# Loading one weight matrix in one transfer of whole rows instead of three transfers by columns

## The chip, the cores and the metric

The kernel runs on one core of a Trainium2 chip. The core has five engines with an instruction stream each: TensorE (PE; its weight loads are shown apart as PEld), VectorE (DVE), ScalarE (ACT), GpSimd (POOL) and SyncE (SP), and 16 DMA engines that all transfers share. The metric is the device time of one launch in microseconds (us). Lower is better.

## What is computed

Sliding-window attention with four sink positions, and then a feed-forward layer that takes the larger of three products:

```python
# q, k, v: (4, 8, 768, 64) float32; n_sink = 4, window = 128
scores = q @ k.T / sqrt(64)
keep = (pos_k < n_sink) | (0 <= pos_q - pos_k < window)
a = softmax(where(keep, scores, -1e9))
x = (a @ v) as (3072, 512)                  # batch and position by heads
h = maximum(maximum(x @ w1, x @ w2), x @ w3)   # w1, w2, w3: (512, 768)
out = h @ w_out                             # w_out: (768, 512), out: (3072, 512) float32
```

## The kernel before

The work is cut into 12 chunks of 256 positions, three to each batch entry. In the code a chunk is `ci`, from 0 to 11. Every chunk goes through the same steps: load q, k and v (`load`, float32, issued on SP), cast them to bf16 on ACT, DVE or POOL (`cast_qk`, `cast_v`), turn q and k so that the head dimension lies on the partitions (`turn`: four TensorE transposes into a PSUM bank and one copy out of it), `score`, `expo`, `mask`, `av`, turn the result (`xpose`), the feed-forward products `ffn_h(ci, fp, wi)` and the last product `ffn_y`. In `ffn_h`, `wi` is the weight matrix (0, 1, 2) and `fp` is the third of its 768 columns: columns 256·fp to 256·fp+255, eight matmuls of 128x256 each.

Nothing schedules this at run time. Lines 626 to 936 write out one order of calls by hand, and every engine executes its own instructions in that order. An engine whose next instruction waits for something executes nothing behind it.

Three things feed the stretch that the change touches.

- **Weights** come in on POOL (`load_w`, line 289). POOL's transfers cast float32 to bf16 on the way, and the weight in memory is 512 rows of 768 columns, so a third of the columns is 512 pieces of 256 float32 (1 KB read, 512 B written). Weights 0, 1 and 2 take three such transfers each, nine in all; `load_wo` brings w_out in two.
- **q, k, v** come in on SP, in pieces of 512 B (two positions of one head). Chunk 2's k and q are loaded in two halves by heads (`part=0`, `part=1`), which are 512 pieces each; its v is 1024.
- **Gates.** `gate=after(wi, c)` and `gate=pool_gate` put a 1x1 instruction on POOL that touches the tile to be loaded, so SP's transfer waits until POOL has reached that place (with `after`, also until that weight has landed).

Around the change the calls stand in this order (lines 697 to 739, the ones that matter): `load(2,'k')` in two halves, `load(2,'q')` in two halves, the loads of weight 2, `ffn_h(0, ...)`, `av(1, ...)`, `load(2,'v')`, `ffn_h(0, fp, 1)`, then

```python
        cast_qk(2, 'k', 1, nc.gpsimd)      # needs the second half of chunk 2's k
        ffn_h(1, 2, 0)
        cast_qk(2, 'k', 0, nc.scalar)      # needs the first half
        ffn_h(1, 0, 0)
        ffn_h(1, 1, 0)
        load_wo()                          # POOL, behind its cast of k
        load(3, 'q', gate=after(2, 300))
        ...
        turn(2, 'k', 0, nc.vector)
        ffn_h(1, 0, 1)
        turn(2, 'k', 1, nc.scalar)
        ffn_h(1, 1, 1)
        ...
        ffn_h(1, 2, 1)
        ffn_h(1, 1, 2)                     # first use of weight 2
```

TensorE takes the two `turn(2, 'k', ...)` at their places between the products, whether or not anything later is ready.

Of the kernel before, what the change touches and what calls it, by code (L numbers as in the profile page):

```python
# [16 lines left out]
def kernel(  # L17
# [31 lines left out]
    with tc.manual_schedule():  # L49
# [43 lines left out]
        def load(ci, what="kqv", gate=None, part=None, parts=1, eng=None):  # L93
            if ci >= NCH:
                return
            b, c = divmod(ci, CPB)
            t0 = c * 256
            for w in what:
                src = {"k": k, "q": q, "v": v}[w]
                if (ci, w) not in raws:  # L100
                    raws[ci, w] = raw.tile([128, H, 2, D], F32, tag=w + "_raw", name=w + "_raw")
                dst = raws[ci, w]
                if gate is not None:
                    gate(dst[0:1, 0, 0, 0:1])
                n = H // parts
                for g in range(parts) if part is None else (part,):
                    (eng or nc.sync).dma_start(
                        out=dst[:, n * g:n * g + n],
                        in_=src[b, n * g:n * g + n, t0:t0 + 256]
                            .rearrange("h (p i) d -> p h (i d)", i=2))  # L110
# [178 lines left out]
        def load_w(wi, c0=0, c1=None):  # L289
            c1 = d_ff if c1 is None else c1  # L290
            w = (moe_w1, moe_w2, moe_w3)[wi]
            nc.gpsimd.dma_start(out=w_sb[wi][:, :, c0:c1],  # L292
                                in_=w.rearrange("(a p) f -> p a f", p=128)[:, :, c0:c1])
# [98 lines left out]
        def expo(ci, p):  # L392
            if ci >= NEW:
                return expo4(ci, p)
            lo = 0 if ci % CPB else 1
            e, st = es[ci, p]
            for a in range(2):
                nc.scalar.activation(e[:, a, lo:], st[a][:, lo:], AF.Exp, scale=scale)  # L398
                give(st[a])

        def mask(ci, p, eng=None):
            if ci >= NEW:
                return mask4(ci, p)
            lo = 0 if ci % CPB else 1
            e = es[ci, p][0]
            (eng or nc.vector).tensor_mul(e[:, :, lo:], e[:, :, lo:], msk0[0] if lo else msk)  # L406
# [295 lines left out]
        score(1, (2,))  # L702
        load(2, 'q', part=1, parts=2)
        load(2, 'q', part=0, parts=2, gate=pool_gate)
        load_w(2, 0, 256)
        expo(1, 2)
        load_w(2, 256, 512)
        load_w(2, 512, 768)
        mask(1, 3)
        ffn_h(0, 1, 0)  # L710
        mask(1, 2)
# [269 lines left out]
```

## Time and profile before

| what | us |
|---|---|
| median of three runs | 175.97 |
| the three runs | 175.69, 175.97, 176.78 |
| the profiled execution's own time | 175.3 |
| its span (first to last event on the core) | 173.6 |
| TensorE busy in that span | 167.1 |
| GpSimd busy | 110.9 |

The span is 1.7 us shorter than the profiled execution's time; that remainder lies around the program. In the profile, "idle before, <- releaser" says how long an engine stood before an instruction and what ended the wait. A wait for several things is put down to the one that came last by the profile; where the engine named had long been done, it was another, often a DMA. Queue q0 (software) carries the transfers that POOL issues, queue q1 (hardware) those that SP and ACT issue. Sizes of packets are counted on the written side, so a weight piece of 1 KB counts as 512 B.

### The profile page before, as it was taken

The page shows a single profiled execution, that of the slowest core. Times are in us where ns is not written, and L with a number is a line of the kernel's source. Part 1 is how long each engine was busy: PE and PEld are TensorE (multiplying, and loading weights), DVE is VectorE, ACT ScalarE, POOL GpSimd, SP SyncE. Part 2 cuts the span into 40 slices and gives each one's busy share as a digit, 9 for nine tenths or more (in the row PEclk, how much of TensorE's full clock was granted, in tenths as well). Part 3 has the DMA queues.
Part 4 walks back from the last instruction along what each step waited for, and adds up shares of the span by engine and source line. Part 5 has one row for each costly group of instructions (what it writes and reads, how often), then busy time and mean ns, then how long its engine had stood idle before and what let it go on. Part 6 is the DMA issues. An engine that isn't in the chain of part 4 may idle for free.

```text
span 173.6 us, 5416 instructions
## 1 busy us (share of the span) xinstructions
PE 167.1 (96%) x2225; PEld 128.6 (74%) x2225; DVE 124.7 (72%) x262; ACT 88.7 (51%) x183; POOL 110.9 (64%) x193
## 2 busy tenths in 40 slices
PE   7979999999999999999999999999999999999992
PEld 2546888857696697797797797797797896896871
DVE  3387854796797985986877976877777776776361
ACT  4778544677954614817726717717636516510210
POOL 7399507545499999999999999999998600000000
PEclk9999999999999999999999999999999999999999
DMA  4999999999999997988999999989999119017303
GB/s 139 301 288 198 218 217 256 221 306 276 280 195 216 190 273 124 245 199 216 253 199 252 195 224 246 265 168 227 264 195 259 32 33 377 21 34 272 121 2 121
DMA packets 71545, 35.22 MB, mean 203 GB/s; under 512 B 27488, under 2 KB 69984, under 8 KB 71520
## 3 DMA queue, kind: packets, MB, share of 16 engines
q1 hardware_dynamic: 65824, 31.60, 79.0%
q0 software_dynamic: 5552, 3.15, 12.7%
q8 instruction: 17, 0.28, 0.7%
q10 hardware_dynamic: 144, 0.13, 0.2%
q14 instruction: 8, 0.07, 0.1%
HBM read 25.17 MB, written 6.29 MB: 181 GB/s over the span
## 4 chain that ended last, share of the span: by engine, by line
PE 85%; DMA 7%; POOL 5%; issue 1%; DVE 0%; POOLq 0%; SPq 0%
PE h_ps L517 52%; PE y_ps L564 11%; PE y_ps L540 7%; PE o L471 6%; DMA w<-in_moe_w_dram 4%; PE st L357 3%; DMA v_raw<-in_v_dram 3%; PE st L331 2%; POOL w L292 2%; POOL vb L123 1%; PE pt L138 1%; PE o L453 1%; PE y_ps L586 1%; PE sk L423 1%; POOL q_bf L118 0%
## 5 line engine op out<-in xcount | busy, mean ns | idle before, releaser
L517 PE MATMUL h_ps<-xT,w 128*128 128x256 bf16 x864 | 101.2, 273 | 0.2 <-DMA w<-in_moe_w_dram 0.2
L517 PEld LDWEIGHTS <-w 128*128 128x128 bf16 x864 | 81.7, 98 | 10.7 <-issue 0.5
L527 DVE TENSOR_TENSOR h_sb<-h_sb,h_ps 128x512 bf16<-128x512 bf16 (+1 forms) x74 | 49.0, 670 | 17.4 <-PE h_ps L517 15.6
L523 ACT CAST h_sb<-h_ps 128x512 bf16<-128x512 f32 x35 | 20.6, 589 | 51.3 <-PE h_ps L517 51.2
L129 POOL CAST vb<-v_raw 32x512 bf16<-32x512 f32 x48 | 36.8, 766 | 2.5 <-DMA v_raw<-in_v_dram 0.3
L90 POOL CAST k_bf<-k_raw 32x512 bf16<-32x512 f32 x48 | 29.6, 616 | 2.2
L398 ACT ACTIVATE e_sb<-st 128x512 bf16<-128x512 f32 (+1 forms) x48 | 23.1, 583 | 1.1 <-PE st L331 1.1
L479 DVE TENSOR_TENSOR x_sb<-o,rc 128x256 bf16<-128x256 f32 x48 | 20.4, 424 | 1.7
L564 PE MATMUL y_ps<-wo,h_sb 64*64 64x512 bf16 (+1 forms) x312 | 21.1, 377 | 0.0
L471 PE MATMUL o<-vb,e_sb 128*128 128x65 bf16 x352 | 16.5, 193 | 0.8 <-DVE vb L123 0.8
L471 PEld LDWEIGHTS <-e_sb 128*128 128x128 bf16 x352 | 14.5, 97 | 3.1 <-ACT e_sb L398 1.0
L123 POOL CAST vb<-v_raw 64x512 bf16<-64x512 f32 x18 | 12.6, 697 | 5.7 <-DMA v_raw<-in_v_dram 5.1
L389 DVE TENSOR_TENSOR e_sb<-e_part,msk 128x1024 bf16<-128x1024 bf16 x16 | 13.1, 831 | 3.3 <-ACT e_part L374 3.1
L406 DVE TENSOR_TENSOR e_sb<-e_sb,msk 128x1024 bf16<-128x1024 bf16 (+1 forms) x18 | 13.6, 776 | 2.3 <-ACT e_sb L398 2.1
L564 PEld LDWEIGHTS <-h_sb 64*64 64x64 bf16 (+1 forms) x312 | 9.9, 106 | 5.0
L374 ACT ACTIVATE e_part<-st 128x384 bf16<-128x384 f32 x32 | 13.1, 495 | 0.5 <-PE st L357 0.5
L540 PE MATMUL y_ps<-wo,h_sb 128*128 128x512 bf16 x54 | 12.8, 380 | 0.0
L476 DVE RECIPROCAL rc<-o 128x4 f32<-128x4 f32 x48 | 8.4, 174 | 4.0 <-PE o L471 3.8
L118 POOL CAST k_bf<-k_raw 128x512 bf16<-128x512 f32 x6 | 3.8, 650 | 9.5 <-PE pt L138 6.8
L118 ACT CAST q_bf<-q_raw 128x512 bf16<-128x512 f32 x13 | 7.6, 620 | 3.0 <-DMA q_raw<-in_q_dram 3.0
L540 PEld LDWEIGHTS <-h_sb 128*128 128x128 bf16 x54 | 4.8, 98 | 5.4 <-DVE h_sb L527 0.8
L427 ACT ACTIVATE e_sink<-sk 128x256 bf16<-128x256 f32 x8 | 3.1, 389 | 10.0 <-PE sk L423 10.0
(90 smaller groups left out, 142.9 us busy)
## 6 DMA issues: line engine op xcount, KB each, us to landing
k_raw<-in_k_dram SPq DMA_DIRECT2D x11, 512.0 KB, 5.6
v_raw<-in_v_dram SPq DMA_DIRECT2D x11, 512.0 KB, 5.6
q_raw<-in_q_dram SPq DMA_DIRECT2D x10, 512.0 KB, 6.9
out_dram<-y_sb SPq DMA_DIRECT2D x9, 512.0 KB, 3.1
w<-in_moe_w_dram POOLq DMA_DIRECT2D x9, 256.0 KB, 6.1
q_raw<-in_q_dram SPq DMA_DIRECT2D x4, 256.0 KB, 7.6
out_dram<-y_sb SPq DMA_DIRECT2D x1, 1024.0 KB, 5.3
wo<-in_moe_w_out_dram POOLq DMA_DIRECT2D x2, 384.0 KB, 8.0
```

What stands on the lines that cost most here:

```text
L90: f(bfs[ci, "k"][x:x + 32, :, n], raws[ci, "k"][y:y + 32, :, i].rearrange("q (p a) d -> q p a d", a=2))
L123: eng.tensor_copy(vb[ci % RING][64 * i:64 * i + 64, n, :, 0:D], raws[ci, "v"][64 * n:64 * n + 64, :, i])
L129: eng.tensor_copy(vb[ci % RING][x:x + 32, n, :, 0:D], raws[ci, "v"][y:y + 32, :, i])
L398: nc.scalar.activation(e[:, a, lo:], st[a][:, lo:], AF.Exp, scale=scale)
L406: (eng or nc.vector).tensor_mul(e[:, :, lo:], e[:, :, lo:], msk0[0] if lo else msk)
L471: nc.tensor.matmul(o[:, t, a], lhsT=e[:, a, s], rhs=vb[cv % RING][:, n, 2 * p + a], start=first, stop=True, skip_group_check=True)
L479: nc.vector.tensor_mul(xs[ci][:, p], o[:, :, :, 0:D], rc.unsqueeze(3).to_broadcast([128, 2, 2, D]))
L517: nc.tensor.matmul(hp[:, f].rearrange("q (i t r) -> q i t r", i=2, r=x.shape[3]), lhsT=w_sb[wi][:, ds, c0:c0 + 128], rhs=x, start=(ds == 0 ...
L523: (nc.scalar.copy if eng is nc.scalar else eng.tensor_copy)(dst, hp)
L527: nc.vector.tensor_max(dst[:, x], dst[:, x], hp[:, x])
L540: nc.tensor.matmul(yp, lhsT=hs[ci][:, fb, t * 128:(t + 1) * 128], rhs=wo[:, fb], start=(fb == 0), stop=(fb == FB - 1))
L564: nc.tensor.matmul(yps[ci][t][c:c + cols], lhsT=hs[ci][hp, fb, x:x + cols], rhs=wo[hp, fb], start=(turn == 0 and fb == 0), stop=(turn == 1 ...
```

## The change

Weight 2 is loaded by one transfer of all 768 columns, at the place in the order where its first third was issued. The other two issues are gone. Weights 0 and 1 and all else stay as they were.

```diff
         load(2, 'q', part=1, parts=2)
         load(2, 'q', part=0, parts=2, gate=pool_gate)
-        load_w(2, 0, 256)
+        load_w(2)
         expo(1, 2)
-        load_w(2, 256, 512)
-        load_w(2, 512, 768)
         mask(1, 3)
         ffn_h(0, 1, 0)
         mask(1, 2)
```

The transfer is now 512 pieces of 768 float32 (3 KB read, 1.5 KB written) where it was 1536 pieces of 1 KB read. The bytes are the same.

On POOL's queue, at the place behind the gate of chunk 2's q (`w_109` is weight 2, `w_107` weight 0; in brackets the counters that an instruction waits for, DMAHW for transfers of SP, DMASW for those of POOL):

```order
 L602 CAST k_raw<-w_107 1x1 [waits DMAHW1_49,DMASW1_49]
 L606 MEMSET q_raw 1x1 [waits DMAHW0_49]
-L292 DMA w_109<-in_moe_w_dram 128x4x256 x2
-L292 DMA w_109<-in_moe_w_dram 128x4x256 [waits DMASW0_49]
+L292 DMA w_109<-in_moe_w_dram 128x4x768
 L602 CAST v_raw<-w_107 1x1 [waits DVE_49]
 L118 CAST k_bf<-k_raw 128x2x2x2x64 [waits DMAHW1_49,PE_49,Pool_49]
 L300 DMA wo<-in_moe_w_out_dram 128x3x512
-L300 DMA wo<-in_moe_w_out_dram 128x3x512 [waits DMASW2_49]
-L602 CAST q_raw<-w_109 1x1 [waits DMASW7_49,Activation_49]
+L300 DMA wo<-in_moe_w_out_dram 128x3x512 [waits DMASW0_49]
+L602 CAST q_raw<-w_109 1x1 [waits DMASW6_49,Activation_49]
```

Two issues go, and everything behind them keeps its order: the gate of chunk 2's v, the cast of the second half of chunk 2's k, the two loads of w_out, the gate of chunk 3's q.

On TensorE, at its first weight load from weight 2 (`ffn_h(1, 1, 2)`):

```order
 L517 LDWEIGHTS w_108
 L517 MATMUL h_ps<-xT,w_108 128x256
-L517 LDWEIGHTS w_109 [waits DMASW7_49]
+L517 LDWEIGHTS w_109 [waits DMASW6_49]
 L517 MATMUL h_ps<-xT,w_109 128x256 [waits PE_49]
 L517 LDWEIGHTS w_109
```

The order of TensorE's instructions is unchanged. Its first use of weight 2 waited for the second of the three transfers, and waits for the one transfer now.

## Prediction

> **What bounds the kernel now.** I read the page's totals and slices first, then the busy time by stages, then the timeline around the change, then single transfers.
>
> ```profile
> span 173.6 us, 5416 instructions
> PE 167.1 (96%) x2225; PEld 128.6 (74%) x2225; DVE 124.7 (72%) x262; ACT 88.7 (51%) x183; POOL 110.9 (64%) x193
> PE   7979999999999999999999999999999999999992
> DMA  4999999999999997988999999989999119017303
> PE 85%; DMA 7%; POOL 5%; issue 1%; DVE 0%; POOLq 0%; SPq 0%
> ```
>
> TensorE is the bound: 96% busy and 85% of the chain that ended last. But the DMA engines are near full as well, from the second slice to the 31st. The stages (columns: stretch, length, busy of PE, PEld, DVE, ACT, POOL, granted clock) show where TensorE has room:
>
> ```profile
> 9.00:15.80 6.80, 5.33 (x88) 3.44 (x86) 5.78 (x16) 5.23 (x12) 6.42 (x11) 1.00 1.29 253
> 22.70:26.40 3.70, 3.67 (x35) 3.28 (x36) 1.48 (x3) 2.08 (x4) 0.00 (x0) 1.00 1.30 216
> 26.40:30.40 4.00, 4.00 (x43) 3.49 (x41) 1.80 (x3) 1.79 (x3) 3.27 (x6) 1.00 1.25 260
> 60.00:170.00 110.00, 110.00 (x1587) 88.49 (x1585) 81.89 (x161) 49.52 (x105) 72.42 (x108) 1.00 0.82 187
> ```
>
> From 22.7 us TensorE has no gap worth naming, so there is next to nothing to win behind that point, and a wait put in there is not made good later: it moves the end by its whole length. The granted clock is 1.00 in every stage, also in the one where TensorE stood for 1.47 us (6.80 - 5.33), so I price no slower clock for a wait of that length.
>
> The timeline of TensorE's weight loads, with POOL and ACT beside them, shows which inputs arrive just in time:
>
> ```profile
> 22.73 3.39 PEld L517 LDWEIGHTS <-w 128*128 128x128 bf16 x32 [0.34 <-DMA w<-in_moe_w_dram]
> 26.13 0.32 PEld L138 LDWEIGHTS <-k_bf 128*128 128x128 bf16 x4
> 27.39 0.23 PEld L138 LDWEIGHTS <-k_bf 128*128 128x128 bf16 x4 [0.17 <-POOL k_bf L118]
> 27.57 2.56 PEld L517 LDWEIGHTS <-w 128*128 128x128 bf16 x24
> 25.17 0.62 ACT L118 CAST k_bf<-k_raw 128x512 bf16<-128x512 f32 x1
> 17.53 2.23 POOL L292 DMA_DIRECT2D w<-in_moe_w_dram  x3
> 26.72 0.61 POOL L118 CAST k_bf<-k_raw 128x512 bf16<-128x512 f32 x1 [6.81 <-PE pt L138]
> 27.28 1.51 POOL L300 DMA_DIRECT2D wo<-in_moe_w_out_dram  x2
> ```
>
> The transposes at 27.39, `turn(2, 'k', 1)`, wait for POOL's cast, which ends at 27.33. That cast had POOL idle for 6.81 us before it. The row blames TensorE's transposes, but the cast stands ahead of chunk 2's transposes in the order and can only wait for those that last used the buffer, long done. So it was the load, and the single transfers bear that out (start from the timeline, last number: us to landing):
>
> ```profile
> 16.59 0.74 POOL L292 DMA_DIRECT2D w<-in_moe_w_dram  x1
> w<-in_moe_w_dram POOLq DMA_DIRECT2D x1, 256.0 KB, 6.1
> w<-in_moe_w_dram POOLq DMA_DIRECT2D x1, 256.0 KB, 7.6
> 17.58 0.92 SPq L107 DMA_DIRECT2D k_raw<-in_k_dram  x2
> k_raw<-in_k_dram SPq DMA_DIRECT2D x1, 256.0 KB, 6.5
> 17.99 0.51 SPq L107 DMA_DIRECT2D k_raw<-in_k_dram  x1
> k_raw<-in_k_dram SPq DMA_DIRECT2D x1, 256.0 KB, 8.6
> 18.27 0.75 POOL L292 DMA_DIRECT2D w<-in_moe_w_dram  x1
> w<-in_moe_w_dram POOLq DMA_DIRECT2D x1, 256.0 KB, 9.7
> ```
>
> The last third of weight 1 (16.59) lands at 22.69, which is what TensorE waits for at 22.73. The thirds of weight 2 start landing at 17.53 + 7.6 = 25.1, the second at 18.27 + 9.7 = 28.0. Chunk 2's k lands at 17.58 + 6.5 = 24.1 (first half) and 17.99 + 8.6 = 26.6 (second half). 26.6 is 0.13 us ahead of POOL's cast at 26.72. **The second half of chunk 2's k is on TensorE's path with about no slack**, and it shares the DMA engines with weight 2.
>
> How they share is in the queues' packets, in windows of 7, 2, 1.2 and 3 us:
>
> ```profile
> q0 software_dynamic: 2720, 1.35, 143.6%
> q0 software_dynamic: 429, 0.22, 77.7%
> q1 hardware_dynamic: 420, 0.21, 52.0%
> q0 software_dynamic: 170, 0.17, 84.1%
> q1 hardware_dynamic: 170, 0.09, 35.3%
> q1 hardware_dynamic: 1730, 0.87, 116.1%
> q0 software_dynamic: 5552, 3.15, 12.7%
> ```
>
> From 13 to 20 us weights run alone: 7000 x 16 / 2720 = 41.2 ns for one piece of 1 KB on one DMA engine. From 22 to 24 us weight 2 and chunk 2's k run together, 429 packets against 420. From 33 to 34.2 us it is w_out with pieces of 2 KB (1 KB written) against the q and k loads: 170 against 170. So the queues take turns **by pieces, whatever their size**. A turn of both costs 2000 x 16 / 424.5 = 75.4 ns with 1 KB pieces and 1200 x 16 / 170 = 112.9 ns with 2 KB pieces. Queue q1 alone (9 to 12 us) takes 3000 x 16 / 1730 = 27.7 ns a piece. The last row, for the whole span, shows pieces uncut: 9 transfers x 512 + 2 x 384 + 11 x 16 (one completion per DMA engine) is 5552 exactly, with w_out's 2 KB pieces counted once.
>
> **The change, part by part.**
>
> *Two issues fewer on POOL.* Three cost 2.23 us, one 0.74 or so: 1.5 us less. POOL then stands idle before its cast of k anyway (6.81 us), and the gate of chunk 2's v, which comes 1.5 us sooner, is followed on SP by a transfer that stands behind the two loads of q. Gain: nothing. If that idle time were gone it would be 1.5 us of POOL's time.
>
> *Weight 2 lands sooner.* It is first needed by `ffn_h(1, 1, 2)`, the last 8 of the 24 weight loads from 27.57, so at about 27.57 + 16 x 0.107 = 29.3 (2.56 / 24 = 0.107); today its second third is there at 28.0. No row shows TensorE waiting for weight 2. Gain: nothing. The gate of chunk 3's q, which now needs the whole weight, is reached at 28.8, behind the landing worked out below.
>
> *Weight 2 takes a larger share while k is on its way.* This is the price. Each DMA engine has 32 pieces of weight 2 (512 / 16) where it had 96, and every turn moves 3 KB instead of 1. No row shows 3 KB pieces; going on from 75.4 and 112.9 ns by the same 37.5 ns per KB, a turn of both takes 150.4 ns. From below, the third KB could be free: 112.9. From above, pieces might cost more the longer they are: three lone 1 KB pieces plus one of q1 make 3 x 41.2 + 27.7 = 151.3, and nothing in the rows goes past that; I allow 170. I take 150.4, with both ends kept.
>
> Clock from 22.69, when the last DMA engine is done with weight 1 (its landing). Check on today: weight 2's first third is 32 turns x 75.4 ns = 2.41 us, landing at 25.10; the row says 25.1. The second half of k lands 26.59 - 22.69 = 3.90 us after that point, so 3.90 / 0.0754 = 51.7 pieces of k go out from there (32 of the second half and some 20 of the first). After the change the first 32 of these take their turns with 3 KB pieces, the rest run alone:
>
> 32 x 150.4 ns + 19.7 x 27.7 ns = 4.81 + 0.55 = 5.36 us, landing at 28.05, **1.46 us later**. Weight 2 itself lands at 22.69 + 4.81 = 27.5 instead of 30.4.
>
> POOL's cast follows at 28.18, ends at 28.79, and the transposes start at 28.85 instead of 27.39: TensorE stands still for 1.46 us. The first half of k lands 1.39 us after that point today, which is 18.4 turns, so it lands at 22.69 + 18.4 x 0.150 = 25.46 instead of 24.1; ACT's cast goes from 25.17 to about 25.6 and ends at 26.2, which TensorE meets at 26.13: up to 0.15 us, which is part of the 1.46, since the later wait is for a fixed moment. Behind POOL's cast the issue of w_out and the gate of chunk 3's q move by the same 1.46 us, and so does everything on TensorE that needs them. Behind the one transfer the loads of q and v have the DMA engines to themselves and catch up: the next half of q lands at 28.05 + 32 x 0.0277 = 28.9; it landed at 18.54 + 10.4 = 28.9 before.
>
> ```profile
> 18.54 1.89 SPq L107 DMA_DIRECT2D q_raw<-in_q_dram  x2
> q_raw<-in_q_dram SPq DMA_DIRECT2D x1, 256.0 KB, 10.4
> ```
>
> Nothing behind that is late against TensorE, and TensorE has no gap in which to win it back. Sum: 0 (POOL) + 0 (weight 2 sooner) + 1.46 = **+1.46 us**, 0.8%. On the profiled execution that is 173.6 + 1.46 = 175.1 of span and 175.3 + 1.46 = 176.8 of time; its own time lies 0.7 us below the median of the runs, 175.97, so the median after is **177.4 us**.
>
> On how the turns are taken, the Trainium skill (DMA: Bandwidth & Descriptors, section "Queues, rings and completion order") says that a DMA engine goes round its queues by whole packets of some 9 to 17 descriptors. The counts above are equal either way, so the rows cannot tell packets from single pieces. Even if all 32 pieces of weight 2 went ahead of k, the second half of k would still have all of them in front of it, and the sum stays what it is.
>
> **The rivals.**
>
> *Not slower: the long rows are cut.* If the transfer is split into pieces of at most 1 or 2 KB read, or the queues share by bytes, k keeps its turns, lands at 26.6, and nothing changes: 176.0. Against it stands the count of 5552, in which 2 KB pieces are whole; for it, that no row shows a longer one. It decides wherever a turn stays under 113 ns, for then k is late by only 0.3 us.
>
> *A gain: one large transfer is cheaper.* What could be won is the wait for weight 1's end (0.34) only if weight 2 were out of its way, which it isn't, and the 0.17 us before the transposes: 175.7 at best. Against it: 2 KB pieces cost 112.9 - 27.7 = 85 ns where two of 1 KB cost 82. The Trainium skill (same page, "Rules for kernel authors") asks for transfers of 1 MiB and more, and its fit of 2.0 us plus bytes over 436 GB/s would estimate one transfer of 1.5 MiB at 5.6 us against 9.6 for three in a row. Here, whatever is saved on weight 2 finds nobody waiting for it.
>
> *Heavier: a 3 KB piece costs more than the line through 1 and 2 KB says.* At 170 ns a turn, 32 x 170 + 19.7 x 27.7 = 5.99 us, k lands at 28.7, 2.1 us later: 178.1. From 160 ns on the loss passes 1%.
>
> *Heavier: w_out is late too.* It is issued behind the cast, at 28.7 instead of 27.3. If its second half then takes all its turns against chunk 3's q (24 x 33 ns = 0.8 us more), half a microsecond of that may reach TensorE: 1.46 + 0.5, 177.9.
>
> **How the numbers follow.** The forecast (+1.1 to +1.9 around 1.46) gets 0.52; rows cut 0.15; a gain 0.05; the heavier piece 0.16; w_out late 0.12. A measurement of this kernel tells about 1% (1.76 us) from no change. 0.12 of the forecast's chance lies past 1%; with the two heavier cases that makes 0.40 for slower. Within 1% are 0.40 of the forecast, 0.15 and 0.02, together 0.57; 0.03 of the gain is left for faster, should the full PE rows hide waits on transfers. The range goes from 175.9, half of the cut rows' case, to 178.6, past both heavier cases, and leaves out some 0.2.
>
> **What would show it.** Right: q0 with 1024 packets fewer; k's second half landing near 28.0; POOL's cast of it at 28.2; about 1.5 us of idle before TensorE's transposes, where 0.17 stands now; chunk 2's later inputs no later than today. Wrong: packets of weight 2 still 512 B; k landing before 27.2; TensorE idle at w_out or chunk 3's q instead; or the span growing by more than that one wait.

## The result and the profile after

| | before | after |
|---|---|---|
| median of 19 runs each, us | 176.11 | 177.43 |
| profiled execution's own time, us | 175.3 | 177.16 |
| its span, us | 173.6 | 175.5 |

The change costs time: ratio 1.0085, 95% interval 1.006 to 1.011. The forecast was 177.4 us. The ratio leaves out disturbed runs, of after the one at 180.92 us, while the medians hold all 19; the other 18 runs of after lie between 176.92 and 179.22. The rows of the page of after that answer to those of before (totals, two rows of slices, shares of the chain, queue q0):

```profile
span 175.5 us, 5410 instructions
PE 168.2 (96%) x2220; PEld 129.1 (74%) x2225; DVE 126.4 (72%) x262; ACT 88.5 (50%) x183; POOL 108.0 (62%) x191
PE   7978998999999999999999999999999999999992
DMA  5999999999998998798899998998999609118203
PE 79%; DMA 12%; POOL 5%; issue 1%; SPq 1%; DVE 0%; POOLq 0%
q0 software_dynamic: 4496, 3.15, 12.0%
```

Queue q0 has 1056 packets fewer for the same bytes: 1024 pieces and the 2 x 16 completions of the two transfers that are gone. So the 3 KB rows are moved whole. In the chain the share of transfers has grown from 7 to 12%. The stages around the change and the long one behind it (columns as before):

```profile
22.70:26.40 3.70, 3.59 (x38) 3.02 (x36) 2.64 (x5) 1.18 (x3) 0.00 (x0) 1.00 1.14 216
26.40:30.40 4.00, 3.55 (x38) 2.98 (x36) 1.11 (x2) 2.48 (x5) 2.00 (x3) 1.00 1.02 275
60.00:170.00 110.00, 109.75 (x1585) 88.66 (x1587) 83.86 (x162) 50.24 (x107) 72.23 (x109) 1.00 0.83 191
```

TensorE was full from 26.4 to 30.4 us before; now it stands 0.45 us in that stage. The clock is 1.00 there and behind. What it stands for is in the timeline of after, with the single transfers (last number: us from issue to landing):

```profile
17.59 0.74 POOL L292 DMA_DIRECT2D w<-in_moe_w_dram  x1
w<-in_moe_w_dram POOLq DMA_DIRECT2D x1, 768.0 KB, 10.4
18.04 0.69 SPq L107 DMA_DIRECT2D k_raw<-in_k_dram  x1
k_raw<-in_k_dram SPq DMA_DIRECT2D x1, 256.0 KB, 10.2
28.40 0.61 POOL L118 CAST k_bf<-k_raw 128x512 bf16<-128x512 f32 x1 [9.91 <-DMA k_raw<-in_k_dram]
27.25 0.32 PEld L138 LDWEIGHTS <-k_bf 128*128 128x128 bf16 x4
29.07 0.23 PEld L138 LDWEIGHTS <-k_bf 128*128 128x128 bf16 x4 [0.73 <-POOL k_bf L118]
29.25 2.34 PEld L517 LDWEIGHTS <-w 128*128 128x128 bf16 x22
```

Chunk 2's k, second half, lands at 18.04 + 10.2 = 28.24 where it was 26.6. POOL's cast starts 0.16 us behind it, and the row now names the transfer. The transposes start at 29.07 instead of 27.39, 1.68 us later; from there to the end of the span it is 175.5 - 29.07 = 146.4 us, against 173.6 - 27.39 = 146.2 before. So nearly the whole difference is there when these four weight loads begin.

Yet only 0.73 us of it is idle time of TensorE's weight loads at this place, 0.56 more than before. The other 1.12 us were there already at the transposes of k's first half, which start at 27.25 here and at 26.13 before, with no wait for k in either row: in this execution TensorE came late to this place for another reason. Had the old transfers met such an execution, would the time have been lost as well? That asked for a second profile of each kernel.

### The profile page after: what moved, and what is told of

Read it like the earlier page. It is cut to its first block, busy times and chain, and to the rows that moved or that the text cites. A ratio compares the mean times of both kernels' runs of the same rounds, so it can differ in the third digit from the quotient of the medians.

```text
span 175.5 us, 5410 instructions
## 1 busy us (share of the span) xinstructions
PE 168.2 (96%) x2220; PEld 129.1 (74%) x2225; DVE 126.4 (72%) x262; ACT 88.5 (50%) x183; POOL 108.0 (62%) x191
## 3 DMA queue, kind: packets, MB, share of 16 engines
q0 software_dynamic: 4496, 3.15, 12.0%
## 4 chain that ended last, share of the span: by engine, by line
PE 79%; DMA 12%; POOL 5%; issue 1%; SPq 1%; DVE 0%; POOLq 0%
PE h_ps L517 49%; PE y_ps L564 11%; DMA k_raw<-in_k_dram 9%; PE o L471 6%; PE y_ps L540 5%; PE st L357 3%; DMA xT<-x_sb 3%; PE st L331 2%; POOL w L292 2%; PE pt L138 1%; PE o L453 1%; POOL k_bf L118 1%; POOL vb L123 1%; PE y_ps L586 1%; SPq L107 1%
## 5 line engine op out<-in xcount | busy, mean ns | idle before, releaser
L90 POOL CAST k_bf<-k_raw 32x512 bf16<-32x512 f32 x48 | 29.1, 607 | 4.2 <-DMA k_raw<-in_k_dram 2.2
L118 POOL CAST k_bf<-k_raw 128x512 bf16<-128x512 f32 x6 | 4.3, 717 | 12.7 <-DMA k_raw<-in_k_dram 12.6
## 6 DMA issues: line engine op xcount, KB each, us to landing
w<-in_moe_w_dram POOLq DMA_DIRECT2D x1, 768.0 KB, 10.4
```

The costliest lines, as they stand in the source:

```text
L90: f(bfs[ci, "k"][x:x + 32, :, n], raws[ci, "k"][y:y + 32, :, i].rearrange("q (p a) d -> q p a d", a=2))
L118: f(x[:, 2 * g:2 * g + 2].rearrange("q p i a d -> q p a i d"), y[:, 4 * g:4 * g + 4].rearrange("q (p a) i d -> q p a i d", a=2))
```

## The experiments

Times of each kernel are compared with runs of the kernel before on the same chip. The diffs are against the changed kernel unless said otherwise. The theory all through: **pieces of 3 KB make each turn of queue q0 long, so chunk 2's k lands late, and TensorE stands before its transposes.**

### Both kernels once more

No edit. First the kernel before:

> The kernel before, profiled once more, nothing changed. The first profile of it, 173.6 us of span, was 0.7 us faster than the median. Theory (the executions differ in the first 16 us, by when TensorE comes up to its full rate): TensorE's first weight load of ffn_h is near 16.2 instead of 15.83, the transposes of the second half of k start between 27.4 and 28.2, and the span is 173.6 to 174.6, with the stretch from these transposes to the end 146.2 us as before. Rival (the executions differ behind 28 us): that stretch is longer by the 0.7 us.

It took 176.09 us, span 174.4. The timeline of this second execution of before, TensorE's weight loads and POOL's cast:

```profile
23.58 3.39 PEld L517 LDWEIGHTS <-w 128*128 128x128 bf16 x32 [0.62 <-DMA w<-in_moe_w_dram]
28.08 0.32 PEld L138 LDWEIGHTS <-k_bf 128*128 128x128 bf16 x4
27.09 0.61 POOL L118 CAST k_bf<-k_raw 128x512 bf16<-128x512 f32 x1 [6.61 <-DMA k_raw<-in_k_dram]
```

TensorE reaches the transposes at 28.08, with k cast since 27.70: no wait for k at all, where the first profile had 0.17 us. The profile on which the prediction rests was an early execution; its own time of 175.3 lies 0.8 us below the median over 19 runs, this one's at it. Then the kernel after:

> The changed kernel, profiled once more, nothing changed. Theory (the second half of k sets the time): whatever the first 16 us, the transposes start at 28.9 to 29.2 and the span is 175.2 to 175.6. Rival (TensorE's early lateness in the first profile of it, 0.8 us at 23.5 us, is part of the loss): with an early start the transposes start near 28.3 and the span is 174.7.

176.99 us, span 175.3. TensorE's weight loads in this second execution of after:

```profile
26.98 0.23 PEld L138 LDWEIGHTS <-k_bf 128*128 128x128 bf16 x4 [0.67 <-ACT k_bf L118]
28.99 0.23 PEld L138 LDWEIGHTS <-k_bf 128*128 128x128 bf16 x4 [1.02 <-POOL k_bf L118]
```

Here TensorE was early, and waits 0.67 us for the first half of k and 1.02 for the second, 1.69 together; the transposes start at 28.99, within 0.1 us of the other execution. **In both executions the changed kernel's end is set by the moment at which k is there**, though TensorE reached the first half of k 0.9 us earlier in the second (26.98 - 0.67 = 26.31, against 27.25). Before, the start of the transposes lies between 27.4 and 28.1, now at 29.0. By the two profiles of each, the mean loss is (177.16 + 176.99)/2 - (175.3 + 176.09)/2 = 1.38 us; the medians of the 19 runs differ by 1.32.

### Three transfers, but 3 KB rows

Is it the one transfer or the long row? Weight 2 in three transfers again, at the three old places, cut by rows instead of by columns:

```diff
-        load_w(2)
+        load_w_rows(2, 0, 2)
         expo(1, 2)
+        load_w_rows(2, 2, 3)
+        load_w_rows(2, 3, 4)
```

(`load_w_rows` loads `w_sb[wi][:, a0:a1]`, all 768 columns.)

> Weight 2 again in three transfers at the three old places, but cut by rows (256, 128 and 128 rows of the full 3 KB), so the pieces are as long as in the changed kernel and the count of transfers is as before. Theory (the length of a piece sets how much queue q0 takes of each turn): the second half of chunk 2's k lands near 28.2 us as in the changed kernel, where it was 26.6, and the time is 1.5 us over the kernel before, 177.5. Rival (it is the one large transfer, or the missing issues on POOL, that costs): k lands at 26.6 and the time is that of before, 176.1.

177.24 us, ratio 1.0078 [1.006, 1.0097]: like the changed kernel. POOL's cast and TensorE's transposes in it:

```profile
28.49 0.61 POOL L118 CAST k_bf<-k_raw 128x512 bf16<-128x512 f32 x1 [8.64 <-DMA k_raw<-in_k_dram]
29.15 0.23 PEld L138 LDWEIGHTS <-k_bf 128*128 128x128 bf16 x4 [0.74 <-POOL k_bf L118]
```

Both rows stand within 0.1 us of the changed kernel's. The number of transfers, and the issues saved on POOL, do nothing here; the length of the piece does it.

### Pieces of 1.5 KB

```diff
-        load_w(2)
+        load_w(2, 0, 384)
         expo(1, 2)
+        load_w(2, 384, 768)
```

> Weight 2 in two transfers of 384 columns, pieces of 1.5 KB. Theory of turns by pieces: a turn lasts halfway between 75 and 113 ns, 94 ns; weight 2 has 64 pieces on a DMA engine, so all 51.7 pieces of k take turns: 22.69 + 51.7 x 0.094 = 27.55, 1.0 us later than before; time +1.0 us, 177.1. Rival (the loss grows evenly with the length of the piece, from 1 to 3 KB): a quarter of 1.5 us, +0.4, 176.5. Rival (only the one whole transfer costs): 176.1.

176.36 us, ratio 1.0025 [1.001, 1.004]. The same two rows:

```profile
27.75 0.61 POOL L118 CAST k_bf<-k_raw 128x512 bf16<-128x512 f32 x1 [8.61 <-DMA k_raw<-in_k_dram]
28.42 0.23 PEld L138 LDWEIGHTS <-k_bf 128*128 128x128 bf16 x4 [0.82 <-POOL k_bf L118]
```

The place is hit: k was expected at 27.55, and the cast starts at 27.75, between those of 1 KB (26.72 and 27.09) and of 3 KB (28.40). So is the turn: from 23 to 26 us each queue moves 511 pieces, 3000 x 16 / 511 = 93.9 ns, where 94 was expected. The time is a miss: 177.1 by the theory, 176.5 by the rival of an even growth, which does better on the time alone. The theory's time was added to the early execution of before. Against the second one, with its start at 28.08, the transposes are late by 0.34 us only, and the time grew by 0.34 (176.36 - 176.02); that the two agree so closely, from one profile of each, is luck.

### Pieces of 512 B

The other way: six transfers of 128 columns, two and four at the old places.

```diff
-        load_w(2)
+        load_w(2, 0, 128)
+        load_w(2, 128, 256)
         expo(1, 2)
+        load_w(2, 256, 384)
+        load_w(2, 384, 512)
+        load_w(2, 512, 640)
+        load_w(2, 640, 768)
```

> The other way: weight 2 in six transfers of 128 columns, pieces of 512 B, at the same places. Two of the added issues also wait for transfers of weight 0 and 1 to land. Theory: a turn lasts about 56 ns (75.4 - 37.5 / 2), the second half of k lands at 22.69 + 51.7 x 0.056 = 25.6, 1.0 us earlier than before, and the transposes no longer wait; weight 2 takes the loss now, its second third is in after 4 x 32 turns, 22.69 + 7.2 = 29.9, and TensorE wants it at 29.2: +0.5 us, 176.6. Rival (pieces' length does not matter): 176.1, with k at 26.6.

176.96 us, ratio 1.0057 [1.0038, 1.0076], 0.4 us more than expected. From 23 to 26 us the queues move 851 and 881 pieces, 3000 x 16 / 866 = 55.4 ns a turn (56 expected). Its timeline, POOL's cast and then TensorE:

```profile
26.00 0.61 POOL L118 CAST k_bf<-k_raw 128x512 bf16<-128x512 f32 x1 [3.73 <-DMA k_raw<-in_k_dram]
27.82 0.32 PEld L138 LDWEIGHTS <-k_bf 128*128 128x128 bf16 x4
30.70 0.33 PEld L517 LDWEIGHTS <-w 128*128 128x128 bf16 x4 [0.49 <-DMA w<-in_moe_w_dram]
39.13 2.10 PE L540 MATMUL y_ps<-wo,h_sb 128*128 128x512 bf16 x9 [0.59 <-DMA wo<-in_moe_w_out_dram]
```

k is 2.4 us earlier than with 3 KB, and TensorE waits for it no more. Now weight 2 itself is late (a wait of 0.49 us), as expected, and w_out behind it (0.59), which the expectation had not named. The size of a piece is a lever with a loss at both ends: it shifts the DMA engines' time from one queue to the other. Over the four sizes, 0.5, 1, 1.5 and 3 KB, the cast starts at 26.0, 26.7 to 27.1, 27.75 and 28.3 to 28.5.

### The transposes two products later

If TensorE's wait is the whole loss, it goes when TensorE has other work until k is there. `turn(2, 'k', 1)` moved behind the next two products of weight 1:

```diff
-        turn(2, 'k', 1, nc.scalar)
         ffn_h(1, 1, 1)
         ...
         ffn_h(1, 2, 1)
+        turn(2, 'k', 1, nc.scalar)
         ffn_h(1, 1, 2)
```

> The changed kernel with one call moved in TensorE's order: the transposes of the second half of chunk 2's k come two products later (behind ffn_h(1, 2, 1) instead of ahead of ffn_h(1, 1, 1)), 2.1 us of work that does not need them. Theory (the loss is TensorE standing before these transposes and nothing else): k still lands near 28.2, TensorE no longer waits, the whole loss is gone: time of the kernel before less its own 0.17 us of wait, 176.0. Rival (what is late behind k, w_out or chunk 3's q, or the larger share itself, costs the time): 177.4 stays.

176.74 us, ratio 1.0062 [1.0035, 1.0089]: a miss for the theory at first sight. TensorE's weight loads and, last, a row of its waits:

```profile
26.85 0.23 PEld L138 LDWEIGHTS <-k_bf 128*128 128x128 bf16 x4 [0.41 <-ACT k_bf L118]
29.60 0.32 PEld L138 LDWEIGHTS <-k_bf 128*128 128x128 bf16 x4
PEld L517 <- DMA xT<-x_sb: 1.1, 1, 1.1
```

The wait for the second half is gone, as wanted, but 0.41 us for the first half and 1.1 us near 58 us, for a transposed x, stand elsewhere (the wait for x is 0.4 to 0.6 us in the profiles of before and after). The rival was that a second loss lies behind the first. So the same kernel was run again:

> The kernel with the late transposes again (0.6% over before the first time), beside the two that follow, so that the three share the runs of the kernel before. Theory of the second loss (POOL issues w_out and chunk 3's q late): 0.4 to 0.7% over before, with a wait of TensorE for the transposing transfer near 58 us of 0.6 us or more. Rival (the first run of it had a disturbed transfer of v, 6.2 us to landing where others take 4): within 0.3% of before, that wait 0.5 us or less.

176.36 us, ratio 1.0007 [0.9987, 1.0026]. Its transposes, from the timeline of TensorE:

```profile
27.11 2.56 PEld L517 LDWEIGHTS <-w 128*128 128x128 bf16 x24
29.67 0.32 PEld L138 LDWEIGHTS <-k_bf 128*128 128x128 bf16 x4
```

No wait here, and no row for x among the waits: the rival's outcome, and not that of a second loss. The two measurements of one kernel disagree (0.6% and 0.1%, intervals apart), and why is left open. They were taken on two chips, each against the kernel before on its own. In the first profile a load of v at 52.20 us took 6.2 us to land where the second's took 4.4, but neither that nor the wait for x is shown to cost the difference: the two profiled executions took 176.53 and 176.51 us, and the products behind x start at 59.50 in the first, after its wait, and at 59.31 in the second. So the move of the transposes alone brought the time back in one measurement of two.

### The cast off POOL as well

In the changed kernel POOL's cast of k stands ahead of the issue of w_out and the gate of chunk 3's q. Here the transposes are moved as above, the cast goes to DVE, and w_out is gated on weight 2's landing instead:

```diff
-        cast_qk(2, 'k', 1, nc.gpsimd)
         ...
+        after(2)(wo[0:1, 0, 0:1])
         load_wo()
         ...
-        turn(2, 'k', 1, nc.scalar)
+        cast_qk(2, 'k', 1, nc.vector)
         ffn_h(1, 1, 1)
         ...
         ffn_h(1, 2, 1)
+        turn(2, 'k', 1, nc.scalar)
```

> The kernel of the late transposes once more, with POOL's issues taken off the wait for k: the cast of the second half of chunk 2's k goes to DVE (ahead of the maximum of ffn_h(1, 1, 1)), and POOL issues w_out as soon as weight 2 has landed (a 1x1 gate), near 28.1 us instead of 28.9. Theory (behind TensorE's wait there is a second loss: POOL issues w_out and chunk 3's q late, the DMA engines run dry between 30 and 32 us, and the loads behind stay late until TensorE waits for a transposing transfer near 58 us): the engines run dry for 0.8 us less, that wait falls by some 0.6 us and the time to 176.1 to 176.3. Rival (that later wait comes from something else): 176.7 stays.

176.18 us, ratio 1.0023 [0.9991, 1.0056]. POOL's gate and issue, and TensorE's transposes:

```profile
28.14 0.18 POOL L602 COPY wo<-w 1x1 bf16<-1x1 bf16 x1 [9.33 <-DMA w<-in_moe_w_dram]
28.61 1.60 POOL L300 DMA_DIRECT2D wo<-in_moe_w_out_dram  x2 [0.30 <-POOL wo L602]
29.55 0.32 PEld L138 LDWEIGHTS <-k_bf 128*128 128x128 bf16 x4
```

w_out goes out at 28.61 instead of 28.96, not the 28.1 hoped for, as the gate costs 0.18 + 0.30 us. The time is the one expected (176.1 to 176.3), and the wait for x fell from 1.1 to 0.4 us. But the stretch from 29 to 32 us, in which the DMA engines run short (last section), moved 0.51 MB, against 0.52 in the first run of the late transposes, so the way in which it was to come about missed. Repeated:

> The kernel with the cast on DVE and w_out issued on weight 2's landing, again, beside the two others. Theory of the second loss: 0.3 to 0.5% faster than the late transposes alone, within 0.3% of before. Rival: the same as the late transposes alone.

175.97 us, ratio 0.9991 [0.997, 1.0011]. That is 0.16% below the late transposes beside it (1.0007), with the intervals overlapping, where 0.3 to 0.5% was expected: a second loss is not shown. **Of the two intervals both hold 1.000, and both end below 1.006, where that of the changed kernel begins**: with the same single transfer, the same 3 KB pieces and k landing no earlier (28.3 in the second run) the loss is gone once TensorE needn't have k at 27.4 to 28.1. No version is shown to beat the kernel before; this one can't be told from it.

### How far the next edge is

Is anything else near? In the kernel of the late transposes, `factors(msk0[0], addm0)`, 1.08 us of POOL's work, moved ahead of the issue of w_out and of chunk 3's q:

```diff
+        factors(msk0[0], addm0)
         load_wo()
         load(3, 'q', gate=after(2, 300))
         load(3, 'k')
-        factors(msk0[0], addm0)
```

> The kernel with the late transposes, with POOL's two mask instructions (1.1 us) put ahead of its issues of w_out and of the gate of chunk 3's q, so that these are issued another 1.1 us later. Theory of the second loss: the loads behind come still later and TensorE waits for it in full or in part, 0.5 to 1.1 us over the kernel with the late transposes, at w_out or at the transposing transfer near 58 us. Rival (their moment does not matter): the same time as that kernel.

177.81 us, ratio 1.0098 [1.0069, 1.0127], 1.45 us over its sister run of 176.36, more than the 0.5 to 1.1 expected. In this kernel, POOL's cast of chunk 3's q and TensorE's transposes of it:

```profile
40.77 0.78 POOL L118 CAST q_bf<-q_raw 128x512 bf16<-128x512 f32 x1 [5.30 <-DMA q_raw<-in_q_dram]
41.59 0.22 PEld L138 LDWEIGHTS <-q_bf 128*128 128x128 bf16 x4 [1.38 <-POOL q_bf L118]
```

The same two rows without that delay:

```profile
39.58 0.77 POOL L118 CAST q_bf<-q_raw 128x512 bf16<-128x512 f32 x1 [3.99 <-DMA q_raw<-in_q_dram]
40.40 0.23 PEld L138 LDWEIGHTS <-q_bf 128*128 128x128 bf16 x4
```

Cast and transposes are both 1.19 us later. So POOL's issues do set when something comes due, but the next input on the edge is chunk 3's q; this expectation had named w_out or the transposing transfer near 58 us. (The prediction had chunk 3's q among its signs of being wrong.) In the changed kernel it costs nothing: there its cast starts at 38.59 and TensorE comes to it at 41.30, late itself by the wait for k.

## Why the prediction was right, step by step

The two views that carry its main term, the packets of both queues from 23 to 26 us, first of the kernel before:

```profile
q0 software_dynamic: 631, 0.31, 75.8%
q1 hardware_dynamic: 635, 0.32, 51.9%
```

and of the kernel after:

```profile
q0 software_dynamic: 310, 0.48, 86.7%
q1 hardware_dynamic: 312, 0.16, 26.2%
```

- *Turns by pieces, whatever their size*: right. 631 against 635 with 1 KB, 310 against 312 with 3 KB; k's queue moves half the bytes it did (0.16 MB for 0.32) in the same 3 us.
- *150.4 ns a turn*: 3000 x 16 / 311 = 154.3 ns (before, 3000 x 16 / 633 = 75.8). Over 32 turns that is 0.12 us more. It stays under the 160 ns from which the rival of a heavier piece would have passed 1%.
- *k at 28.05, 5.36 us after weight 1's end*: 28.24, which is 5.4 us after that end (22.84). Cast forecast for 28.18, measured 28.40; transposes forecast for 28.85, measured 29.07 and 28.99.
- *Weight 2 sooner, and nobody gains*: it landed at 17.59 + 10.4 = 28.0, which is 0.5 us behind the forecast of 27.5 (0.15 of it from weight 1's later end, 0.12 from the longer turn, the rest not explained), and no wait for it stands in either profile of before or after. POOL's idle time before its cast grew from 6.81 to 9.91 us, so the issues saved are worth nothing, as said.
- *The first half of k, up to 0.15 us*: too small. It landed at 25.6 and 26.2 in the two profiles of after, where 25.46 was forecast, and the wait for it is 0.67 us in the second. It adds nothing to the end, as the prediction said: the second wait is for a fixed moment.
- *About 1.5 us of idle before the transposes*: failed as a sign, 0.73 and 1.02 us. The step behind it was to take TensorE's arrival of one execution for a constant. It varies by 0.86 us between the two profiles of before (27.39 - 0.17 = 27.22, and 28.08). What holds still in the two profiles of after is the start of the transposes, and that was forecast within 0.25 us.
- *Median = profile's time + 1.46 + 0.7*: the mechanism is right, but that 177.4 meets 177.43 so closely is luck. The median of before is 176.11 and not the 175.97 of three runs, and the medians differ by 1.32 and not by 1.46: two errors of 0.14 us that cancel. Nor does each execution lose the same: against the early first profile of before the transposes start 1.68 us later, against the second 0.9 to 1.0. Both profiles of after lie below its median, by 0.27 and 0.44 us, and what its slower runs, up to 179.2, lose beyond the wait for k is not shown.
- *No slower clock for the wait*: right, the stage reads 1.00 after the change. The 1.47 us that the prediction leaned on were several waits, though, the longest of them 0.8 us of PE.
- *Nothing is late behind it*: right for the changed kernel; the stretch behind the transposes is 146.4 and 146.3 us. Of chunk 2's later inputs the first half of q landed 0.2 us later than before (29.2, forecast 28.9), v 0.5 us sooner. The rival of a late w_out didn't come true: its two halves landed at 33.9 and 36.2, at 34.3 and 37.0 before. (The prediction doesn't say where that rival's 33 ns a turn come from.) The experiment with the delayed issues shows that it was near for another input, chunk 3's q.
- *The rivals of cut rows and of a gain*: out, the first by the 4496 packets, the second by the time. The Trainium skill (DMA: Bandwidth & Descriptors, section "Rules for kernel authors") asks for 1 MiB and more per transfer for bandwidth. Here weight 2 in one transfer did land 2.4 us sooner than the 30.4 given for before, and the kernel took 0.85% longer: the rule speaks of one transfer, and the wait was for another. The 5.6 us that the prediction estimated for one transfer stand against 10.4 measured, issued behind weight 1 and beside k.

## What to carry to other kernels

Two queues shared the DMA engines here, and the length of a contiguous piece on one set the speed of the other: a turn of both took 55, 76, 94 and 154 ns with pieces of 0.5, 1, 1.5 and 3 KB. So before making a bulk load's rows longer, look which small load is in flight beside it and whether an engine waits for that one. There is a loss on both sides: of the four lengths 1 KB was the best, 1.5 and 3 KB cost 0.25% and 0.85% as k came late, and 512 B cost 0.57% as the bulk load itself came late. An input that lands just in time has no slack for this. Moving its first use two products back, with its cast taken off POOL, gave the time of before in both measurements; the move alone did so in one of two.

## What was not expected of the hardware

**The first microseconds are not the same in each execution.** TensorE's four last warm-up products, from the timelines of the first profile of before, then of after:

```profile
4.91 1.03 PE L203 MATMUL warm<-wz 128*128 128x512 bf16 x4
15.83 0.78 PEld L517 LDWEIGHTS <-w 128*128 128x128 bf16 x8 [0.17 <-issue]
```

```profile
5.08 1.91 PE L203 MATMUL warm<-wz 128*128 128x512 bf16 x4
17.00 0.78 PEld L517 LDWEIGHTS <-w 128*128 128x128 bf16 x8 [0.16 <-issue]
```

The same four matmuls took 1.03 us in one and 1.91 in the other, and the first products with weight 0 start 1.17 us apart, before the change plays any part. The second profiles had 1.91 us (before) and 1.26 (after), so this is the execution, not the kernel. How much of the 1.17 us comes from these matmuls is not shown: the second profile of before spent 1.91 us on them as well and started the same products at 16.40. The granted clock reads 1.00 from the first slice in all of them and doesn't show it. The Trainium skill (TensorE: Matmul & The Clock Gate, section "Part 1: The HAM clock gate") says that a free-running window of some 3.4 us decides when the first matmuls reach full speed, and that the number of matmuls ahead of it varies from run to run; durations that differ by 1.85 times agree with that, though the granted clock doesn't confirm it and no run here varied it on purpose.

**The DMA engines ran short behind the change.** Packets from 29 to 32 us, before and then after:

```profile
DMA packets 1394, 0.84 MB, mean 280 GB/s; under 512 B 32, under 2 KB 1394, under 8 KB 1394
```

```profile
DMA packets 742, 0.44 MB, mean 146 GB/s; under 512 B 18, under 2 KB 742, under 8 KB 742
```

Weight 2 is through by 28.0, and what would follow it, w_out on POOL's queue and chunk 3's q on SP's behind POOL's gate, is issued only behind the late cast, from 28.96 on. Nearly half of three microseconds' transfers is lost there. That it cost nothing is read from the profiles alone: the stretch behind the transposes is as long as before, and TensorE was late by as much as its inputs.
